# Scores of the late batches behind U, in the free columns of two PSUM banks, and five order changes

## The chip, the cores and the metric

The kernel runs on one core of a Trainium2 chip, as one launch. The metric is the device time of a run in microseconds, as the median of the runs shown. Besides that one execution was profiled: its trace holds every instruction of TensorE (PE; its weight loads are PEld), VectorE (DVE), ScalarE (ACT), GpSimd (POOL) and of the queue of SyncE (SP), with start and duration.

## The reference

Eight batches of eight heads, 576 positions of 64 values, are attended over 32 memory slots; the result goes through a gated feed-forward layer.

```python
a = exp(phi - max(phi, axis=2)); a = a / (sum(a, axis=2) + 1e-9)
k_m, v_m = einsum('bhsm,bhsd->bhmd', a, k), einsum('bhsm,bhsd->bhmd', a, v)
scores = q @ k_m.T / 8;  attn = softmax(scores, axis=-1)      # over 32 slots
x = (attn @ v_m) as (4608 tokens, 512)
out = (1 / (1 + exp(-(x @ w_gate))) * (x @ w_val)) @ w_out    # 512 -> 1536 -> 512
```

All is fp32 to the outside. Inside, the large products are made of three products of hi and lo parts.

## The kernel before

`attn @ v_m @ w` is not made in that order: for each batch, U is the product of the memory's values v_m with the weights (both gates), and what the layer needs is `attn @ U`. The feed-forward width is cut into 12 f tiles of 128. Batches 0 to 2 (below `QUAD`) run in a first part of the program, batches 3 to 7, the late ones, in a second part, batch by batch and f tile by f tile; the change lies in the second part but for `KEEP_W`. There the order of all engines is written out by hand: each call of `step` is put behind the one before it on each engine, so the order of calls in the loop over (b, f) is the order of the instructions.

For one f tile of one late batch, the object g (class `Group`) holds two gates of 288 + 288 positions, made by seven half-size products instead of eight (a scheme with sums of operands). Each product is three matmuls of 288 columns. Products 1, 6, 7 and 4 add up in one PSUM bank, called d for even f and b for odd f; product 2 goes to bank a, 5 and 3 to bank c. Of a bank's 512 columns the group uses 288. ScalarE copies partial results out of the banks (`copy`: `c_s<-d` behind product 1, `c_p<-c`, `c_x<-d`), VectorE adds (`add`: `z<-a,c_s`, `z<-c,c_x`, and the third, `z<-d,c_p` or `z<-b,c_p`, that is add(3)), ScalarE applies the sigmoid (`gate`), VectorE multiplies (`product_of`), and the result g is cut into `g_hi` (ScalarE) and `g_lo` (VectorE). One f tile later it is multiplied by w_out: an out tile is three matmuls of 512 columns into one of four accumulators, `acc`. A group's last two products, 7 and 4, are made in the next tile's step: h is the group of the tile before.

A step of the loop stands in this order on TensorE: h's product 7, g's product 1, then in even tiles U for the next two f tiles (`pair_u`, 16 matmuls in the 64*32 shape, `a<-ring,vT` and `c<-ring,vT`, into whole banks a and c, that ScalarE copies out), in some odd tiles work of the next batch (place "m"), one or two out tiles, products 2 and 5, sometimes an out tile, h's product 4, g's product 6, an out tile, product 3, an out tile. The dictionary `plan`, made by `late_sides(b)`, says what work of the next batch n = b + 1 is put at which place of which tile: `put(f, place, ...)`.

The scores of batch n are such work. Before, two pieces of 288 positions are made at f = 3 and f = 5 (place "m", `scores`), in the 64*32 shape, heads in turn into banks a and c; a piece is one part of 256 and one of 32 columns (`a<-q,kT`). VectorE transposes both banks into the tile e (`to_blocks`, place "m3"), takes the maximum over the slots (`s_max`, place "Z" of the same tile) and subtracts it (place "B" of the next). ScalarE takes the exponential of all of e at f = 6, and at f = 8 VectorE sums, inverts and multiplies (`normalize`). A tile with work at "m" is `wide`: it has two out tiles in front of product 2.

Other places that the change touches: `KEEP_W` says at which steps of the first part the converted weights are written to DRAM (two subtractions on VectorE and four DMAs on SP's queue for each entry); `leave_late` takes finished accumulators out (in batch 3 by VectorE, with rows that a DMA brings; later by ScalarE); the last step of all makes product 7 of its own group too.

Of the kernel before, what the change touches and what calls it, by code (L numbers as in the profile page):

```python
# [17 lines left out]
P = 128  # L18
B, H, S, D, M = 8, 8, 576, 64, 32
DM, DFF = 512, 1536  # L20
NG = 2
NKT = 4
NFT = DFF // P
SF = 4
# [3 lines left out]
HALF = S // 2  # L28
EDGE = TAIL // 2
HALVES = [slice(0, HALF), slice(HALF, S)]  # L30
ORDER = [list(range(H)), [2, 3, 0, 1, 6, 7, 4, 5]]
SCALE = 1.0 / 8.0
EPS = 1e-9
# [68 lines left out]
def attn_moe_kernel(  # L102
# [91 lines left out]
    def matmul(*args, **kw):  # L194
        in_turn(nc.tensor.matmul, *args, **kw)
# [274 lines left out]

    def cut(b, c):

        return slice(0, S) if c is None else (CUT if b < QUAD else HALVES)[c]

    def scores(b, c):

        n = cut(b, c).stop - cut(b, c).start
        pb = [late_bank("a"), late_bank("c")] if "banks" in pools else [bank(), bank()]
        if b < QUAD:
            parts = [(u * NKT * 2 * P, nu, 0, nu) for u, nu in PIECES[c]]  # L480
        else:
            parts = [(c * NKT * 2 * P, 2 * P, 0, 2 * P), (NKT * SF * P, TAIL, c * EDGE, EDGE)]
        o = 0
        for at_u, nu, at_c, nc_ in parts:
            qt = loaded[b, "q"][:, at_u : at_u + NKT * nu].rearrange("p (k n) -> p k n", k=NKT)
            for p in range(H):
                rs, l = of_head(b, 0, p)
                js = slice((p // 2) * M, (p // 2 + 1) * M)
                r = qt[rs, p // 2, at_c : at_c + nc_]
                matmul(pb[p % 2][js, o : o + nc_], l, r, start=True, stop=True)  # L490
            o += nc_
        loaded[b, c, "pb"] = [t[:, :n] for t in pb]

# [385 lines left out]

    spare = ident.bitcast(mybir.dt.bfloat16)  # L880
    idle = [po.tile([P, 512], F32, name=f"acc{SF - 1}")]
    memories = {b: memory(b) for b in range(QUAD)}
    is_start = {(b, f): at_start for b, f, at_start, _ in steps}

# [134 lines left out]
            yield  # L1019

    MAIN = begin[QUAD, 0]
    KEEP_W = {17: 0, 18: 1, 19: 2, 20: 3, 22: 4, 25: 5}
    sides = {
        begin[0, TURN]: [(6, remember(QUAD, True))],
        begin[1, NFT - TURN]: [(3, pause(3)), (3, score(QUAD, QUAD + 1))],
# [113 lines left out]
    def late_bank(name):  # L1139
        return pools["banks"].tile([P, 512], F32, name=name)  # L1140

    class Group:
# [19 lines left out]
        def p(self, n):  # L1162
            where, x, t, start = {
                1: ("d", "a11", "b11", True), 2: ("a", "a12", "b21", True), 5: ("c", "s1", "t1", True),
                6: ("d", "s2", "t2", False), 3: ("c", "s4", "b22", False), 7: ("d", "s3", "t3", False),
                4: ("d", "a22", "t4", False),
            }[n]
            if start:
                name = "b" if where == "d" and self.f % 2 else where
                setattr(self, where, late_bank(name)[:, :HALF])  # L1170
            self.product(getattr(self, where), x, t, start)
            if self.f == NFT - 1:
                free_rooms.append(room_of_at.pop((self.b, t)))

        def copy(self, name):
            nc.scalar.copy(getattr(self, name), self.c if name == "p5" else self.d)  # L1176

        def add(self, i):
            x, y = {0: (self.a, self.s1), 1: (self.c, self.x), 3: (self.d, self.p5)}[i]
# [132 lines left out]
    def late_sides(b):  # L1312
# [4 lines left out]
        def put(f, place, do, *args):  # L1317
            plan.setdefault((f, place), []).append((do, args))
# [5 lines left out]
        if n < B:  # L1324
            if n > QUAD + 1:
                put(0, "m2", go, n)
                put(0, "end", go, n, 2)
            soft = [s_max(n, c) for c in range(2)]
            norm = normalize(n)
            for c in range(2):  # L1330
                put(2 * c + 3, "m", scores, n, c)
                put(2 * c + 3, "m3", to_blocks, n, c)
                put(2 * c + 3, "Z", next, soft[c])
                put(2 * c + 4, "B", next, soft[c])
            put(6, "act3", s_exp, n)
            put(8, "E", next, norm)
            put(8, "Z", next, norm)
            put(9, "Z", cross, n)
            put(10, "B", sums_at, n, 1, 2)
            put(10, "act2", at_hi, n, "b11")  # L1340
            put(10, "Z", at_lo, n, "b11")
            put(11, "m", at_hi, n, "b21")
            put(11, "E", sums_at, n, 3, 4)
            put(11, "B", at_lo, n, "b21")
            put(11, "x", at_hi, n, "t1")
            put(11, "B2", at_lo, n, "t1")
            put(11, "act2", at_hi, n, "t2")
            put(11, "Z", at_lo, n, "t2")
# [39 lines left out]
    for b, f in [(b, f) for b in range(QUAD, B) for f in range(NFT)]:  # L1388
# [8 lines left out]
        odd = f % 2  # L1397
        more = n + 1 < NPAIRS
        g = Group(b, f)
        g.tiles()  # L1400
        if h:
            step(h.p, 7)
# [8 lines left out]
        wide = (b, f) in LEFT_AT and f != 5 or (f, "m") in plan and (f != NFT - 1 or b + 2 < B) or not odd and more  # L1411
        if not odd and more:
            step(pair_u, n + 1, [late_bank("c"), late_bank("a")])
            step(u_out, n + 1, "r")
            step(u_out, n + 1, "l")
        gated_late = bool(gates)
# [55 lines left out]
        if odd and more:  # L1472
            step(part_hi, n + 1, "s")
        step(g.add, 1)
        step(leave_late)
        if late_left:
            step(next, extra, None)
        last = b == B - 1 and f == NFT - 1
        if last:
            step(g.p, 7)  # L1480
            step(g.add, 3)
        if h:
            step(h.to_lo)
        side("B2")
        gates.extend([(g.gate, 0), (g.gate, 1)])
# [88 lines left out]
```

## Time and profile before

| | |
|---|---|
| median of 3 runs | 718.01 us (717.53 to 718.19) |
| the profiled execution, its own time | 717.56 us |
| span of its instructions | 715.8 us |
| TensorE, VectorE, ScalarE busy | 707.1 us (99%), 552.4 us (77%), 446.7 us (62%) |
| granted TensorE clock | 1.00 |
| chain that ended last, by engine | PE 92%, DMA 3%, ACT 2%, DVE 1% |
| loads of q, issue to landing | 16 of 512 KB, median 4.8 us |

Times in a timeline count from the span's start. A row gives start, duration, engine, line of the kernel, operation, out<-in, shape, type and count. Matmuls are pipelined, so a row's duration is longer than the time to the next start; how much TensorE a matmul takes is read from one start to the next. The same holds, by less, for VectorE and ScalarE.

### The profile page before, as it was taken

Reading aid. Unit: us, or ns where it says so; the run is one execution under the profiler, and the core shown is the slowest. Engines: PE = TensorE matmul, PEld = TensorE weight load, DVE = VectorE, ACT = ScalarE, POOL = GpSimd, SP = SyncE. Lnnn points to the kernel's source line nnn. Section 1 sums busy time; section 2 is a strip of 40 time slices with the busy share of each in tenths; the row PEclk is TensorE's granted clock in tenths of the full one; section 3 lists DMA queues with packets and bytes.
Section 4 is the critical chain, followed back from the end, with each engine's and each line's share of the span. In section 5 each row is a group of like instructions: output and inputs, shape, how many; then the busy total and the mean of one; then the engine's idle time right before and its main releaser. Section 6 shows DMA issues by size and latency. Waiting matters only on the chain.

```text
span 715.8 us, 14239 instructions
## 1 busy us (share of the span) xinstructions
PE 707.1 (99%) x5517; PEld 579.0 (81%) x5517; DVE 552.4 (77%) x1090; ACT 446.7 (62%) x1034; POOL 27.7 (4%) x55
## 2 busy tenths in 40 slices
PE   9999999999999999999999999999999999999997
PEld 7655898888988888878888888887888788888886
DVE  5898998778697675587887779777797777977663
ACT  4755776543354454567877667875777657686553
POOL 0000100111101110100000000000000000000000
PEclk9999999999999999999999999999999999999999
DMA  8966559878976535632176113652313422151102
GB/s 348 405 260 220 203 196 375 305 255 270 319 242 200 213 136 193 243 136 73 60 257 210 60 60 119 225 185 74 111 67 134 148 81 74 60 177 60 60 1 73
DMA packets 36083, 123.21 MB, mean 172 GB/s; under 512 B 3952, under 2 KB 11376, under 8 KB 28848
## 3 DMA queue, kind: packets, MB, share of 16 engines
q1 hardware_dynamic: 31296, 106.71, 42.3%
q0 software_dynamic: 4560, 15.47, 6.1%
q8 instruction: 43, 0.70, 0.4%
q14 instruction: 24, 0.20, 0.1%
q10 hardware_dynamic: 160, 0.13, 0.1%
HBM read 96.73 MB, written 25.56 MB: 171 GB/s over the span
## 4 chain that ended last, share of the span: by engine, by line
PE 92%; DMA 3%; ACT 2%; DVE 1%; SPq 1%; issue 0%; DVEq 0%; ACTq 0%
PE acc L192 39%; PE pu_t L192 20%; PE c L192 11%; PE a L192 9%; PE b L192 7%; PE d L192 7%; DMA kvm<-in_kvm_dram 2%; DMA words<-in_wo_dram 1%; SPq L178 1%; ACT L162 0%; DVE e L508 0%; DVE e L499 0%; ACT e L167 0%; ACT sg L167 0%; DVE mx L506 0%
## 5 line engine op out<-in xcount | busy, mean ns | idle before, releaser
L192 PE MATMUL acc<-wo_hi,g_hi 128*128 128x512 f32 x372 | 152.1, 409 | 0.0
L192 PE MATMUL acc<-wo_hi,g_lo 128*128 128x512 f32 x372 | 147.1, 395 | 0.0
L192 PE MATMUL acc<-wo_lo,g_hi 128*128 128x512 f32 x372 | 146.6, 394 | 0.0
L192 PE MATMUL pu_t<-at,u_hi 128*128 128x320 f32 (+1 forms) x560 | 116.5, 304 | 0.0
L192 PEld LDWEIGHTS acc<-wo_hi,g_hi 128*128 128x128 f32 x372 | 69.8, 188 | 37.5 <-ACT c_s L1176 16.8
L192 PEld LDWEIGHTS pu_t<-at,u_hi 128*128 128x128 f32 x560 | 92.1, 188 | 8.4 <-issue 2.1
L192 PEld LDWEIGHTS acc<-wo_hi,g_lo 128*128 128x128 f32 x372 | 69.8, 188 | 17.4 <-DVE g_lo L182 0.8
L192 PE MATMUL pu_t<-at,u_lo 128*128 128x256 f32 (+1 forms) x264 | 77.5, 294 | 0.0
L192 PEld LDWEIGHTS acc<-wo_lo,g_hi 128*128 128x128 f32 x372 | 70.0, 188 | 5.8
L1176 ACT COPY c_p<-c 128x288 f32<-128x288 f32 x60 | 24.0, 399 | 67.7 <-PE c L192 67.0
L167 ACT ACTIVATE sg<-pu_t 128x256 f32<-128x256 f32 (+1 forms) x70 | 28.6, 411 | 50.1 <-PE pu_t L192 45.7
L1180 DVE TENSOR_TENSOR z<-c,c_x 128x288 f32<-128x288 f32 x60 | 27.3, 456 | 34.7 <-PE c L192 31.8
L1180 DVE TENSOR_TENSOR z<-a,c_s 128x288 f32<-128x288 f32 x60 | 27.2, 453 | 34.4 <-PE a L192 32.4
L167 ACT ACTIVATE z<-z 128x288 f32<-128x288 f32 x120 | 48.1, 439 | 8.5 <-DVE z L1180 7.6
L696 DVE TENSOR_TENSOR sg<-pu_t,sg 128x320 f32<-128x320 f32 (+1 forms) x69 | 31.1, 453 | 24.8 <-ACT sg L167 14.8
L706 ACT CAST g_hi<-sg 128x256 fp32r<-128x256 f32 x66 | 26.5, 405 | 37.5 <-DVE sg L696 35.6
L192 PEld LDWEIGHTS pu_t<-at,u_lo 128*128 128x128 f32 x264 | 49.6, 188 | 0.0
L1192 ACT CAST g_hi<-z 128x512 fp32r<-128x512 f32 x60 | 37.3, 622 | 10.0 <-DVE z L1187 10.0
L182 DVE TENSOR_TENSOR g_lo<-z,g_hi 128x512 fp32r<-128x512 f32 x60 | 40.9, 682 | 1.4 <-ACT g_hi L1192 1.3
L1187 DVE TENSOR_TENSOR z<-z 128x288 f32<-128x288 f32 x60 | 27.2, 453 | 6.0 <-ACT z L167 1.1
L192 PE MATMUL a<-ring,vT 64*32 64x512 f32 x232 | 31.4, 601 | 0.0
L192 PE MATMUL c<-ring,vT 64*32 64x512 f32 x232 | 31.4, 601 | 0.0
(242 smaller groups left out, 1623.8 us busy)
## 6 DMA issues: line engine op xcount, KB each, us to landing
ring<-wgv SPq DMA_DIRECT2D x30, 1024.0 KB, 4.9
kvm<-in_kvm_dram SPq DMA_DIRECT2D x14, 1024.0 KB, 9.0
at<-at SPq DMA_DIRECT2D x18, 576.0 KB, 7.7
q<-in_qT_dram SPq DMA_DIRECT2D x16, 512.0 KB, 4.8
part<-row POOLq DMA_DIRECT2D x24, 256.0 KB, 4.9
row<-part SPq DMA_DIRECT2D x24, 256.0 KB, 3.9
words<-in_wo_dram SPq DMA_DIRECT2D x8, 512.0 KB, 9.8
words<-in_wgv_dram SPq DMA_DIRECT2D x4, 1024.0 KB, 5.1
```

The source lines that it names most:

```text
L167: last_act[0] = nc.scalar.activation(*args, **kw)
L178: last_move[queue] = queues[queue].dma_start(dst, src)
L182: return nc.vector.tensor_tensor(lo, x, hi.bitcast(F32), op=ALU.subtract)
L192: last_pe[0] = do(*args, **kw)
L696: last_prod[0] = nc.vector.tensor_tensor(prod, ps[1][:, :n], sg[:, :n], op=ALU.mult)
L706: nc.scalar.copy(hi, prod[:, : 2 * P])
L1176: nc.scalar.copy(getattr(self, name), self.c if name == "p5" else self.d)
L1180: nc.vector.tensor_tensor(self.z[:, i], x, y, op=ALU.add)
L1187: nc.vector.tensor_tensor(self.z[:, 2 + i], x, self.z[:, i], op=ALU.mult)
L1192: nc.scalar.copy(self.g[0], self.z[:, 2:4, : 2 * P])
```

## The change

The scores of batches 4 to 7 (n above `QUAD`) are cut into three pieces of 224, 224 and 128 positions (`ROOMFULS`), since a bank has 224 free columns beside a group's 288. They are made at f = 2, 4 and 6, at a new place "u" directly behind `pair_u`, heads in turn into the free columns of the bank of the tile before (b) and of this tile (d); `now` holds the two groups, and `beside` is the free part of a group's bank. These matmuls don't start an accumulation (`start=False`). Positions 224 to 448 lie over the border of the two halves, so the second piece has three parts (32, 32 and 160 columns), the third two (96 and 32). Tiles 3 and 5 are no longer `wide`. The maximum comes at "Z" of the same tile, the subtraction at "B" of the next, the exponential in two parts at f = 6 and 7.

The five order changes: the weights of pair 4 are kept at step 27 instead of 22; the copy `c_s` of f = 7 in batch 3 is made by VectorE; the product by the inverse sums goes from "Z" of f = 8 to "E" of f = 9 in batch 6; in batch 3 the lo part of h is made ahead of the rows that leave; and in the last step it is made ahead of the last third sum.

```diff
+ROOM = 512 - HALF
+ROOMFULS = [slice(o, min(o + ROOM, S)) for o in range(0, S, ROOM)]
...
     def cut(b, c):
-        return slice(0, S) if c is None else (CUT if b < QUAD else HALVES)[c]
+        if c is None or isinstance(c, slice):
+            return c or slice(0, S)
+        return (CUT if b < QUAD else HALVES if b == QUAD else ROOMFULS)[c]
...
-        pb = [late_bank("a"), late_bank("c")] if "banks" in pools else [bank(), bank()]
+        late = b > QUAD
+        pb = [unit.beside for unit in now] if late else [bank(), bank()]
...
-            parts = [(c * NKT * 2 * P, 2 * P, 0, 2 * P), (NKT * SF * P, TAIL, c * EDGE, EDGE)]
+            parts, cs = [], cut(b, c)
+            for k, half in enumerate(HALVES):
+                edge = half.stop - EDGE
+                for at_u, nu, first, a, z in (
+                    (k * NKT * 2 * P, 2 * P, 0, half.start, edge), (NKT * SF * P, TAIL, k * EDGE, edge, half.stop),
+                ):
+                    lo, hi = max(a, cs.start), min(z, cs.stop)
+                    if lo < hi:
+                        parts.append((at_u, nu, first + lo - a, hi - lo))
...
-                matmul(pb[p % 2][js, o : o + nc_], l, r, start=True, stop=True)
+                matmul(pb[p % 2][js, o : o + nc_], l, r, start=not late, stop=True, skip_group_check=late)
...
-    KEEP_W = {17: 0, 18: 1, 19: 2, 20: 3, 22: 4, 25: 5}
+    KEEP_W = {17: 0, 18: 1, 19: 2, 20: 3, 25: 5, 27: 4}
...
-                setattr(self, where, late_bank(name)[:, :HALF])
+                whole = late_bank(name)
+                setattr(self, where, whole[:, :HALF])
+                if where == "d":
+                    self.beside = whole[:, HALF:]
...
-            nc.scalar.copy(getattr(self, name), self.c if name == "p5" else self.d)
+            late_exp = name == "s1" and self.b == QUAD and self.f == 7
+            copy = nc.vector.tensor_copy if late_exp else nc.scalar.copy
+            copy(getattr(self, name), self.c if name == "p5" else self.d)
...
-            for c in range(2):
-                put(2 * c + 3, "m", scores, n, c)
-                put(2 * c + 3, "m3", to_blocks, n, c)
-                put(2 * c + 3, "Z", next, soft[c])
-                put(2 * c + 4, "B", next, soft[c])
-            put(6, "act3", s_exp, n)
+            for c in range(len(ROOMFULS)):
+                put(2 * c + 2, "u", scores, n, c)
+                put(2 * c + 2, "m3", to_blocks, n, c)
+                put(2 * c + 2, "Z", next, soft[c])
+                put(2 * c + 3, "B", next, soft[c])
+            put(6, "act3", s_exp, n, slice(0, 2 * ROOM))
+            put(7, "act3", s_exp, n, 2)
             put(8, "E", next, norm)
-            put(8, "Z", next, norm)
+            put(*((8, "Z") if m < B else (9, "E")), next, norm)
...
         g = Group(b, f)
+        now[:] = [now[1], g]
...
             step(pair_u, n + 1, [late_bank("c"), late_bank("a")])
+            side("u")
             step(u_out, n + 1, "r")
...
         step(g.add, 1)
+        to_lo_done = h and b == QUAD and leaving
+        if to_lo_done:
+            step(h.to_lo)
         step(leave_late)
...
         if last:
+            step(h.to_lo)
             step(g.p, 7)
             step(g.add, 3)
-        if h:
+        elif h and not to_lo_done:
             step(h.to_lo)
```

TensorE in batch 4 at f = 2, behind U, in the changed program; the waits name the engine's count that a matmul waits for (DVE is VectorE's, Activation ScalarE's, DMAHW a DMA queue's):

```order
L194 MATMUL c<-ring,vT 32x512
L194 MATMUL a<-ring,vT 32x512
L194 MATMUL b<-q,kT 32x224 [waits DMAHW0_49,DVE_49]
L194 MATMUL d<-q,kT 32x224 [waits Activation_49]
L194 MATMUL b<-q,kT 32x224
L194 MATMUL d<-q,kT 32x224
L194 MATMUL b<-q,kT 32x224
L194 MATMUL d<-q,kT 32x224
L194 MATMUL b<-q,kT 32x224
L194 MATMUL d<-q,kT 32x224
L194 MATMUL acc_4834<-wo_hi,g_hi 128x512
```

Before, the out product stood directly behind U, and the scores stood in the next tile. The counts waited for are those of the third sum of the tile before (`z<-b,c_p`) and of the copy `c_s<-d`.

VectorE in batch 3 from f = 1 to f = 2, before, and then after:

```order
L1180 TENSOR_TENSOR z<-c,c_x 128x288 [waits PE_49,Activation_49]
L756 TENSOR_TENSOR row<-acc_3397,row 128x512 [waits DMAHW3_49,DMASW1_49]
L756 TENSOR_TENSOR row<-acc_3401,row 128x512 [waits DMAHW4_49,DMASW2_49]
L182 TENSOR_TENSOR g_lo<-z,g_hi 128x512 [waits Activation_49]
L182 TENSOR_TENSOR u_lo<-s_raw,u_hi 128x768 [waits Activation_49]
L1180 TENSOR_TENSOR z<-b,c_p_3699 128x288 [waits PE_49]
```

```order
L1199 TENSOR_TENSOR z<-c,c_x 128x288 [waits PE_49,Activation_49]
L184 TENSOR_TENSOR g_lo<-z,g_hi 128x512 [waits Activation_49]
L769 TENSOR_TENSOR row<-acc_3397,row 128x512 [waits DMAHW3_49,DMASW1_49]
L769 TENSOR_TENSOR row<-acc_3401,row 128x512 [waits DMAHW4_49,DMASW2_49]
L184 TENSOR_TENSOR g_lo<-z,g_hi 128x512 [waits DVE_49]
L184 TENSOR_TENSOR u_lo<-s_raw,u_hi 128x768 [waits Activation_49]
L1199 TENSOR_TENSOR z<-b,c_p_3699 128x288 [waits PE_49]
```

One g_lo is added in front of the two rows, and the one behind them is still there.

VectorE in batch 4 from the end of f = 3 into f = 4, before, and then after:

```order
L1180 TENSOR_TENSOR z<-c,c_x 128x288 [waits PE_49,Activation_49]
L182 TENSOR_TENSOR g_lo<-z,g_hi 128x512 [waits Activation_49]
L182 TENSOR_TENSOR s_lo<-s_raw,s_hi 128x768 [waits Activation_49]
L506 TENSOR_REDUCE mx<-e 128x2x9
L1180 TENSOR_TENSOR z<-b,c_p_4861 128x288 [waits PE_49]
L1187 TENSOR_TENSOR z<-z 128x288 [waits DVE_49,Activation_49]
```

```order
L1199 TENSOR_TENSOR z<-c,c_x 128x288 [waits PE_49,Activation_49]
L184 TENSOR_TENSOR g_lo<-z,g_hi 128x512 [waits Activation_49]
L184 TENSOR_TENSOR s_lo<-s_raw,s_hi 128x768 [waits Activation_49]
L1199 TENSOR_TENSOR z<-b,c_p_4893 128x288 [waits PE_49]
L512 STREAM_TRANSPOSE e<-b 128x224 [waits PE_49]
L512 STREAM_TRANSPOSE e<-d 128x224 [waits PE_49,Activation_49]
```

The maximum in front of the third sum is gone from here (it stands at the end of f = 2, 4 and 6 now), and two transposes follow the sum.

## Rows read from the trace of the kernel before

**Rows 1.** The page: an engine's busy time, share of the span, instructions.

```profile
PE 707.1 (99%) x5517; PEld 579.0 (81%) x5517; DVE 552.4 (77%) x1090; ACT 446.7 (62%) x1034; POOL 27.7 (4%) x55
```

**Rows 2.** Timeline, TensorE, batch 4, f = 3: one piece of the scores.

```profile
390.58 0.43 PE L192 MATMUL b<-at,u_hi 128*128 128x288 f32 x2
390.85 0.29 PE L192 MATMUL b<-at,u_lo 128*128 128x288 f32 x1
391.08 0.40 PE L192 MATMUL a<-q,kT 64*32 64x256 f32 x1
...
391.53 0.19 PE L192 MATMUL a<-q,kT 64*32 64x32 f32 x1
...
391.73 0.50 PE L192 MATMUL acc<-wo_hi,g_hi 128*128 128x512 f32 x1
392.07 0.40 PE L192 MATMUL acc<-wo_lo,g_hi 128*128 128x512 f32 x1
```

**Rows 3.** Timeline, all engines, batch 4, f = 2: U, third sum, copy.

```profile
384.30 0.61 PE L192 MATMUL c<-ring,vT 64*32 64x512 f32 x1
...
384.83 0.45 DVE L1180 TENSOR_TENSOR z<-b,c_p 128x288 f32<-128x288 f32 x1
385.16 0.40 ACT L1176 COPY c_s<-d 128x288 f32<-128x288 f32 x1
```

**Rows 4.** Timeline, all engines, batch 4, f = 4: U and VectorE's maximum.

```profile
397.50 0.61 PE L192 MATMUL c<-ring,vT 64*32 64x512 f32 x1
...
398.03 0.75 DVE L506 TENSOR_REDUCE mx<-e 128x18 f32<-128x576 f32 x1
```

**Rows 5.** Timeline, all engines, batch 4, f = 6: U and VectorE's maximum.

```profile
413.52 0.61 PE L192 MATMUL c<-ring,vT 64*32 64x512 f32 x1
...
414.65 0.74 DVE L506 TENSOR_REDUCE mx<-e 128x18 f32<-128x576 f32 x1
```

**Rows 6.** Timeline, all engines, batch 3, end of f = 1 into f = 2.

```profile
303.41 0.62 ACT L1192 CAST g_hi<-z 128x512 fp32r<-128x512 f32 x1 [0.78 <-DVE z L1187]
...
303.76 1.28 DVE L756 TENSOR_TENSOR row<-acc,row 128x512 f32<-128x512 f32 x2
...
304.02 0.61 PE L192 MATMUL c<-ring,vT 64*32 64x512 f32 x1
...
304.95 0.68 DVE L182 TENSOR_TENSOR g_lo<-z,g_hi 128x512 fp32r<-128x512 f32 x1
...
305.55 0.95 DVE L182 TENSOR_TENSOR u_lo<-s_raw,u_hi 128x768 fp32r<-128x768 f32 x1
...
306.42 0.45 DVE L1180 TENSOR_TENSOR z<-b,c_p 128x288 f32<-128x288 f32 x1
```

**Rows 7.** Timeline, TensorE, batch 3, f = 7.

```profile
339.79 0.29 PE L192 MATMUL d<-at,u_lo 128*128 128x288 f32 x1
340.14 0.53 PE L192 MATMUL b<-at,u_hi 128*128 128x288 f32 x2
```

**Rows 8.** Timeline, all engines, batch 6, f = 9.

```profile
607.88 0.45 DVE L1180 TENSOR_TENSOR z<-d,c_p 128x288 f32<-128x288 f32 x1
608.02 0.40 PE L192 MATMUL acc<-wo_hi,g_lo 128*128 128x512 f32 x1
608.38 0.53 PE L192 MATMUL d<-at,s_hi 128*128 128x288 f32 x2
```

**Rows 9.** Timeline, TensorE, batch 7, last step.

```profile
702.63 0.39 PE L192 MATMUL acc<-wo_hi,g_hi 128*128 128x512 f32 x1
702.86 0.39 PE L192 MATMUL acc<-wo_lo,g_hi 128*128 128x512 f32 x1
703.27 0.50 PE L192 MATMUL acc<-wo_hi,g_lo 128*128 128x512 f32 x1
```

**Rows 10.** Timeline: VectorE, a weight subtraction; SP's queue, q's loads of batch 5.

```profile
220.10 0.68 DVE L1226 TENSOR_TENSOR row<-wg 64x512 f32<-64x512 f32 x1 [0.60 <-DMA part<-row]
...
378.89 1.28 SPq L178 DMA_DIRECT2D q<-in_qT_dram  x3
```

More of the change, by code (lines that the diff above doesn't have):

```diff
@@ L881, in attn_moe_kernel @@
     idle = [po.tile([P, 512], F32, name=f"acc{SF - 1}")]
+    now = [None, None]
     memories = {b: memory(b) for b in range(QUAD)}
@@ L1327, in late_sides @@
                 put(0, "end", go, n, 2)
-            soft = [s_max(n, c) for c in range(2)]
+            soft = [s_max(n, c) for c in range(len(ROOMFULS))]
             norm = normalize(n)
-            for c in range(2):
-                put(2 * c + 3, "m", scores, n, c)
-                put(2 * c + 3, "m3", to_blocks, n, c)
-                put(2 * c + 3, "Z", next, soft[c])
-                put(2 * c + 4, "B", next, soft[c])
-            put(6, "act3", s_exp, n)
+            for c in range(len(ROOMFULS)):
[5 more added lines that the diff above has]
+            put(7, "act3", s_exp, n, 2)
             put(8, "E", next, norm)
-            put(8, "Z", next, norm)
+            put(*((8, "Z") if m < B else (9, "E")), next, norm)
             put(9, "Z", cross, n)
```

## The prediction

> **What bounds the kernel now.** I read the page first: the reader is to see that TensorE is busy for 99% of the span while VectorE and ScalarE are not [rows 1], and, in the table, that the chain of work that ended last runs almost wholly through TensorE. Then TensorE's timeline inside batches 3 to 7, the part that the change touches. There the matmuls stand back to back: a 288-column one starts 0.13 us after the last (390.58 to 390.85 for two), a 512-column one 0.23 us after it [rows 2, 9]. So time is gained only where TensorE is made to do less or to wait less, and every wait that is added on TensorE is paid in full, since the matmuls behind it are taken in the program's order. Two kinds of loss are seen in the rows. One is the trip into the 64*32 shape and back. The other is a handful of places where the next matmul starts late because VectorE or ScalarE is late [rows 7 to 9]; there the matmul behind the late one loses another 0.10 us (0.53 for the pair instead of 0.43, and 0.50 instead of 0.39).
>
> **The scores leave their own trips.** Before, one piece of the scores costs TensorE the time from 390.98 (390.85 and 0.13) to 391.84 (392.07 less 0.23), 0.86 us [rows 2, 9]; a batch has two, 1.72. After, the three pieces stand behind U, which is in the same shape, so they pay no entry (390.98 to 391.08, 0.10), no exit and no loss behind it. What stays is the streaming: 256 columns take 0.45 for both passes, so 576 take 1.01. A part of 32 columns costs more than its columns: 391.53 to 391.73 is 0.20, 0.10 without an exit like the entry, against 0.06 by columns; three such parts (before: two) add 0.13. So 1.14 instead of 1.72, 0.58 a batch, and 2.3 us for the four batches (4 to 7). Bounds: three short parts at 0.20 each leave 1.1 us of gain; none of the surcharge makes it 2.8.
>
> **What the scores wait for now.** This is the term that decides. The pieces are written into the free columns of banks d and b, and the built program makes the first matmul into each wait, as the rows in the section on the change show: for b on a VectorE count, which is the third sum of the group before (`z<-b,c_p`), for d on a ScalarE count, which is the copy `c_s<-d`. Both only read the first 288 columns, but the wait is there, and behind the waiting matmul stand all out products of the tile. Before, U was followed by out products that needed neither. So the question at each of the twelve places (four batches, f of 2, 4, 6) is whether those two are done when U ends. U is two rounds of 512 columns, 0.90 by the rate above. A release takes 0.05 (the sum that starts at 607.88 ends at 608.33, and the matmul that waits for it starts at 608.38) [rows 8].
> - f = 2, batch 4: U starts at 384.30 and ends at 385.20; the sum ends at 385.28, the copy, late behind the copies of the finished rows, at 385.56 [rows 3]. Wait until 385.61: 0.41 us.
> - f = 4, batch 4: U ends at 398.40. The sum stood behind a maximum; that maximum now comes a tile earlier, so the sum starts where it started, at 398.03, and ends at 398.48 [rows 4]. Wait 0.13 us.
> - f = 6, batch 4: U ends at 414.42. Here VectorE also copies the leftover sums ahead of it. Without the maximum the sum starts at 414.65 and ends at 415.10 [rows 5]. Wait 0.73 us.
> - Batches 5 and 6 repeat these three places with the same distances; 1.27 us a batch, 3.8 for three.
> - f = 2, batch 3: here VectorE adds the finished rows of batch 2. The edit that puts the lo part of g ahead of them does so, but its guard is the list of rows itself, which is empty by the time that it is asked again, so the old lo part stays as well: VectorE does it twice, as the order shows. The chain: g_hi is there at 304.03, the first lo part starts at 304.08 and takes 0.60 (304.95 to 305.55), the two rows 1.19 (303.76 to 304.95), the second lo part 0.60, the lo part of U 0.87 (305.55 to 306.42), the sum 0.45 [rows 6]. It ends at 307.78, and TensorE may start at 307.83; U ends at 304.92. Wait 2.9 us.
> - f = 4 and 6, batch 3: a maximum goes as in rows 4, and there are no leftovers; 0.13 each.
> Sum: 2.9, 0.3 and 3.8, so 7.0 us. What a wait costs beyond itself no row shows for this shape; it lies between nothing and the 0.10 seen for full-size matmuls [rows 7, 8], for twelve places 0 to 1.2. I take 0.4, nearer to nothing, since the loads in the 64*32 shape are short and the shape doesn't change.
>
> The built program waits by bank. The Trainium skill has the rule for it, in PSUM — Partial Sum Buffer, section "PSUM bank collisions raise a hardware error": two engines must be kept apart by bank and quadrant, a different address in the same bank still collides. No row of the kernel before shows two engines in one bank at once. By that rule the waits can't be left out, and the time is the forecast's; if columns alone counted, it would be the first rival's.
>
> **The other edits.** The copy on VectorE (f = 7 of batch 3) takes away the wait at 340.14: 0.22 (339.92 to 340.14) and 0.10 behind it [rows 7]; VectorE is not late there. Moving the product by the inverse sums one step on, behind the sum `z<-d,c_p` that it held up, takes away the wait at 608.38: 0.13 and 0.10 [rows 8]. The lo part ahead of the last third sum takes away that at 703.27: 0.18 (703.09 to 703.27) and 0.11 [rows 9]. Together 0.84 us, if all go; 0 if what comes next is as late. The exponential in two parts adds one short instruction to ScalarE, at f = 7, where it is ahead of the tile's sigmoids by a table load: 0. The 16 further small VectorE instructions (transposes and maxima) stand between waits for TensorE, on an engine that is 77% busy: 0. The weights kept at step 27 instead of 22 move two VectorE subtractions of 0.68 [rows 10] and four DMAs on SP's queue. TensorE shows no wait at the old place, so nothing is gained; at the new one they lengthen a busy run of VectorE by 1.2 us, of which TensorE sees between 0 and 1.2. I take 0, as a lag of three halves is between the two engines there. On SP's queue the DMAs now stand ahead of batch 3's loads of q and of two sets of row loads, whose users come a tile or more later: 0. In the late batches q is needed a tile earlier: issued at 378.89 [rows 10], its first piece, the only one that f = 2 reads, has 6.3 us until 385.20, and the median load takes 4.8 (table): 0.
>
> **The sum.** From the profiled execution's own 717.56: less 2.3, less 0.84, plus 7.0, plus 0.4 gives 721.8, 4.3 us more. The median of the runs, 718.01, lies 0.45 above the profiled execution; I put half of that on top: 722.0 us.
>
> **The rivals.**
> 1. The free columns are free in time: the sum and the copy end before U does, so no wait shows and the gains alone stand: 718.0 less 3.1, 714.9 us. For it: at f = 4 the sum is late by a tenth only, and anything that makes VectorE 0.15 us quicker or TensorE later hides that. Against it: at f = 6 it is late by 0.7 and at batch 3 by 2.9, and VectorE's chain starts when TensorE's last product into c ends, so it is late by the same amount however TensorE is delayed. It decides where the `z<-b,c_p` ends ahead of U's last matmul. Chance 0.10.
> 2. Only the long wait of batch 3 remains, and the others are hidden: the gains of 3.1 and the loss of 2.9 cancel, 717.9 us. It needs the copies of finished rows at f = 2 and the leftovers at f = 6 to fall elsewhere than before; the order shows them at the same places. Chance 0.08.
> 3. The waits cost more than themselves: each re-pays 0.10 (1.2 in all), and VectorE's subtractions at step 27 reach TensorE: 723.5 to 724.5 us. Chance 0.14.
> 4. The forecast: waits as worked out, 720 to 723.4 us. Chance 0.68.
>
> **How the numbers follow.** This kernel's runs differ by 0.2%, 1.4 us, so that is what I call no change. Slower by more than that holds the forecast nearly whole and the third rival: 0.80. No change is the second rival and the edge of the forecast: 0.10. Faster is the first rival: 0.10. The range holds 8 in 10 if it reaches from 717.2 (just under the second rival) to 724.2 (the third's upper part); what it leaves out is the first rival and a little above. The forecast's own range is 720 to 723.4.
>
> **What would show it.** In TensorE's timeline of the changed kernel: the first matmul of `b<-q,kT` starts late behind U's last, by some 2.9 us in batch 3 at f = 2, 0.4 at f = 2 of the other batches (the second one, into d, there), 0.1 at f = 4 and 0.7 at f = 6, each just behind the end of `z<-b,c_p` or `c_s<-d`; two g_lo in a row of four on VectorE in batch 3; no 64*32 matmuls at odd f; and U to the next out product without a second entry. The waits at 340, 608 and 703 are gone. I am wrong if the score matmuls start within 0.05 of U's end at most places, if the gain of the trips is not near 0.58 a batch, or if a wait of over 0.5 us shows at a place that I didn't name.

## The result, and the profile after

| | before | after |
|---|---|---|
| median of the runs | 718.03 us (717.53 to 718.19, 4 runs) | 726.56 us (725.42 to 726.89, 4 runs) |
| the profiled execution, span | 717.56 us, 715.8 us | 726.36 us, 724.6 us |
| second U of the late part (batch 3, f = 0) to the span's end | 422.31 us | 431.31 us |
| granted TensorE clock | 1.00 | 0.998 |

The ratio is 1.0123, 95% interval 1.0111 to 1.0135: slower, as forecast, but by 8.5 us and not by 4.0, above the top of the range (724.2). The third row of the table is what I compare kernels by below. The opening moves single executions by up to 1.2 us (that U starts between 293.0 and 294.2 us in the kernels of this study), while the same program repeats the rest within a few hundredths (420.72 and 420.74 in two profiles of one kernel).

The page of the changed kernel, busy time and the chain that ended last:

```profile
PE 708.6 (98%) x5645; PEld 580.2 (80%) x5645; DVE 556.2 (77%) x1108; ACT 446.1 (62%) x1037; POOL 27.6 (4%) x55
...
PE 85%; DVE 7%; DMA 3%; ACT 3%; issue 1%; SPq 1%; DVEq 0%
```

Beside [rows 1], TensorE is busy for 1.5 us more, which is not the 8.8 that the span grew by: the rest is waiting. The chain says for whom: VectorE's share went from 1% to 7%. The view of waits names it, TensorE's waits from 303 to 620 us (waited for: us in total, times, longest); the same view of the kernel before has no line:

```profile
PE b L194 <- DVE z L1199: 6.7, 9, 2.7
```

Nine of the twelve score places wait for the third sum. The three others, f = 2 of batches 4 to 6, wait in the second matmul, for the copy, and don't show in this view. Here are the places of batches 3 and 4, in the timelines that answer to [rows 3 to 6].

Batch 3, f = 2, TensorE and then VectorE (start, duration, engine, line, operation; a trailing bracket is idle time and its releaser):

```profile
303.85 0.61 PE L194 MATMUL c<-ring,vT 64*32 64x512 f32 x1
...
307.67 0.37 PE L194 MATMUL b<-q,kT 64*32 64x224 f32 x1 [2.73 <-DVE z L1199]
...
308.21 0.51 PE L194 MATMUL acc<-wo_hi,g_hi 128*128 128x512 f32 x1
```

```profile
303.89 0.69 DVE L184 TENSOR_TENSOR g_lo<-z,g_hi 128x512 fp32r<-128x512 f32 x1 [0.22 <-ACT g_hi L1211]
304.50 1.28 DVE L769 TENSOR_TENSOR row<-acc,row 128x512 f32<-128x512 f32 x2
305.69 0.68 DVE L184 TENSOR_TENSOR g_lo<-z,g_hi 128x512 fp32r<-128x512 f32 x1
306.29 0.95 DVE L184 TENSOR_TENSOR u_lo<-s_raw,u_hi 128x768 fp32r<-128x768 f32 x1
307.16 0.45 DVE L1199 TENSOR_TENSOR z<-b,c_p 128x288 f32<-128x288 f32 x1
```

The row of [rows 6] with one g_lo more, as forecast: the sum ends at 307.61, the scores start 0.06 later, 2.9 us after U's end at 304.75.

What I had not forecast stands behind that wait. TensorE by stretches (length, busy, granted clock, DMA share, GB/s), and two matmuls of the stretch:

```profile
304.00:306.80 2.80, 0.94 (x16) 1.00 0.35 38
306.80:309.00 2.20, 1.33 (x19) 0.98 0.93 305
309.00:310.00 1.00, 1.00 (x4) 0.50 0.70 250
...
312.00:313.00 1.00, 1.00 (x8) 0.84 0.00 0
```

```profile
309.09 0.63 PE L194 MATMUL acc<-wo_hi,g_hi 128*128 128x512 f32 x1
309.52 0.63 PE L194 MATMUL acc<-wo_lo,g_hi 128*128 128x512 f32 x1
```

The granted clock is the lower of its two levels, 1.2 instead of 2.4 GHz, from about 308.9 to 312.3 us, and a 512-column matmul takes 0.43 from start to start there, not 0.23.

Batch 4, f = 4, VectorE from the end of f = 3, and then TensorE:

```profile
399.76 0.61 DVE L521 TENSOR_TENSOR e<-e,mx 128x448 f32<-128x448 f32 x1
400.29 0.45 DVE L1206 TENSOR_TENSOR z<-d,z 128x288 f32<-128x288 f32 x1
...
401.43 0.69 DVE L184 TENSOR_TENSOR g_lo<-z,g_hi 128x512 fp32r<-128x512 f32 x1 [0.32 <-ACT g_hi L1211]
402.31 0.96 DVE L184 TENSOR_TENSOR s_lo<-s_raw,s_hi 128x768 fp32r<-128x768 f32 x1 [0.19 <-ACT s_hi L1136]
403.18 0.45 DVE L1199 TENSOR_TENSOR z<-b,c_p 128x288 f32<-128x288 f32 x1
```

```profile
401.86 0.61 PE L194 MATMUL c<-ring,vT 64*32 64x512 f32 x1
...
403.69 0.21 PE L194 MATMUL b<-q,kT 64*32 64x32 f32 x1 [0.74 <-DVE z L1199]
...
404.45 0.50 PE L194 MATMUL acc<-wo_hi,g_hi 128*128 128x512 f32 x1
```

In [rows 4] the maximum started 0.53 after U, and I let the sum start there. It starts 1.32 after U (403.18 less 401.86), and the scores wait 0.93, not 0.13. The new row in this stretch is the subtraction at 399.76. The same stretch of the kernel before, where U starts at 397.50, has none:

```profile
394.87 0.45 DVE L1187 TENSOR_TENSOR z<-d,z 128x288 f32<-128x288 f32 x1
396.19 0.46 DVE L1180 TENSOR_TENSOR z<-c,c_x 128x288 f32<-128x288 f32 x1 [0.86 <-PE c L192]
```

The gate product `z<-d,z` starts 2.63 ahead of U there and 1.57 ahead of it now, so 1.06 later against U. What hangs on it runs through ScalarE: g_hi reads it, s_hi stands behind g_hi in ScalarE's order, and VectorE's g_lo and s_lo read those two; the third sum stands behind s_lo. The last link before the change, and g_hi now:

```profile
396.03 0.83 ACT L1122 CAST s_hi<-s_raw 128x768 fp32r<-128x768 f32 x1
397.16 0.95 DVE L182 TENSOR_TENSOR s_lo<-s_raw,s_hi 128x768 fp32r<-128x768 f32 x1
```

```profile
400.77 0.62 ACT L1211 CAST g_hi<-z 128x512 fp32r<-128x512 f32 x1 [0.98 <-DVE z L1206]
```

Before, s_hi ended at 396.86, 0.30 ahead of the s_lo that reads it: that was the room of this chain. Now g_hi waits for the gate product, g_lo for g_hi and s_lo for s_hi (0.98, 0.32 and 0.19), and the sum comes 0.79 later (1.32 for 0.53). The 0.86 us that VectorE was idle in front of `z<-c,c_x` is no measure of that room: there it waited for TensorE, and the chain doesn't run through it.

Batch 4, f = 2, TensorE and ScalarE, and f = 6, TensorE and VectorE, as forecast from [rows 3, 5]:

```profile
388.69 0.61 PE L194 MATMUL c<-ring,vT 64*32 64x512 f32 x1
...
389.73 0.56 PE L194 MATMUL b<-q,kT 64*32 64x224 f32 x2
390.01 0.37 PE L194 MATMUL d<-q,kT 64*32 64x224 f32 x1
```

```profile
389.55 0.40 ACT L1195 COPY c_s<-d 128x288 f32<-128x288 f32 x1
```

```profile
420.24 0.27 PE L194 MATMUL b<-q,kT 64*32 64x96 f32 x1 [0.54 <-DVE z L1199]
```

```profile
417.68 0.68 DVE L831 COPY wo_raw<-a 128x512 f32<-128x512 f32 x1
...
419.74 0.45 DVE L1199 TENSOR_TENSOR z<-b,c_p 128x288 f32<-128x288 f32 x1
```

At f = 2 the first matmul into d starts 0.06 after the end of the copy (389.95). At f = 6 the leftover sums' copy still stands ahead of g_lo, the lo part and the sum; the sum ends at 420.19, and the scores start 0.05 later, 0.73 after U's end (U starts at 418.62).

### The profile page after: what moved, and what is told of

The parts are those of the page before. It is cut to its first block, busy times and chain, and to the rows that moved or that the text cites. A ratio compares the mean times of both kernels' runs of the same rounds, so it can differ in the third digit from the quotient of the medians.

```text
span 724.6 us, 14507 instructions
## 1 busy us (share of the span) xinstructions
PE 708.6 (98%) x5645; PEld 580.2 (80%) x5645; DVE 556.2 (77%) x1108; ACT 446.1 (62%) x1037; POOL 27.6 (4%) x55
## 4 chain that ended last, share of the span: by engine, by line
PE 85%; DVE 7%; DMA 3%; ACT 3%; issue 1%; SPq 1%; DVEq 0%
PE acc L194 36%; PE pu_t L194 20%; PE c L194 9%; PE a L194 8%; PE b L194 6%; PE d L194 6%; DMA kvm<-in_kvm_dram 2%; DVE z L1199 1%; DMA words<-in_wo_dram 1%; DVE s_lo L184 1%; DVE u_lo L184 1%; ACT g_hi L1211 1%; SPq L180 1%; DVE e L521 1%; ACT s_hi L1136 1%
```

## The experiments

All are compared by the time from the second U to the end (before 422.31, after 431.31 us), which comes from one profiled execution of each kernel, with the medians beside it. Medians of the kernel before on these chips were 717.3 to 717.6 us.

**The subtraction back in the even tile.**

```diff
-                put(2 * c + 3, "B", next, soft[c])
+                put(2 * c + (4 if c < 2 else 3), "B", next, soft[c])
```

> The changed kernel, but the subtraction of the maximum of the first two score pieces stands in the next even tile (f = 4 and 6, where it stood before the change) and no longer in the odd tile (f = 3 and 5), ahead of the odd tile's gate product. Theory 1 (order on VectorE): in the odd tile the subtraction, 0.61 us, pushes back the chain gate product, g_hi, g_lo, s_lo, third sum, so that at f = 4 the scores wait 0.48 or 0.93 us instead of 0.13. Without it the third sum starts at U + 0.53, the first b<-q,kT at U + 1.03, at f = 4 of batches 3 to 6 and f = 6 of batch 3; three times 0.35 and twice 0.80, so 2.65 us less: 723.9. Theory 2 (more and smaller VectorE instructions, the transposes and maxima of three pieces, make it late): the waits stay at 0.48 and 0.93 and the time at 726.5 within 0.4.

Measured: 724.76 us (ratio to before 1.0101, 1.0082 to 1.0121), 429.48 us, 1.83 less than after. Half a hit. VectorE in batch 4 from f = 3 to f = 4, U at 401.67:

```profile
399.56 0.45 DVE L1206 TENSOR_TENSOR z<-d,z 128x288 f32<-128x288 f32 x1
...
402.47 0.45 DVE L1199 TENSOR_TENSOR z<-b,c_p 128x288 f32<-128x288 f32 x1
```

The gate product comes 0.54 earlier against U (2.11 ahead of it) and the sum starts 0.80 after U instead of 1.32. But it does not come back to 0.53: the wait is 0.40 at f = 4 of batches 3 to 5, and 0.13 only at f = 6 of batch 3 and f = 4 of batch 6. So the subtraction is most of it. For the rest the rows show two things in f = 2: at its end the first piece's maximum (0.61) now stands behind the maximum over positions of the batch after next, which batch 6 does not have; and the sum of product 2, which started 3.19 us after U in the kernel before, starts 3.94 after it here, since the piece and its wait now stand ahead of product 2. Neither was tried alone.

**The lo part of batch 3 made once.**

```diff
-        to_lo_done = h and b == QUAD and leaving
+        to_lo_done = bool(h and b == QUAD and leaving)
```

> The changed kernel, with the guard of the lo part in batch 3 read once as true or false, so that g_lo is made once there, ahead of the rows, and not again behind them. Theory 1: the wait of the scores at f = 2 of batch 3 is VectorE's row of four; one g_lo less makes it 2.3 us instead of 2.9, and the granted clock behind it still falls: 725.9. Theory 2: the clock falls only behind a wait as long as 2.9; then the half-rate stretch behind it goes too, another 1.7 less: 724.2. Theory 3: the second g_lo is hidden (the sum waits for something else): 726.5.

Measured: 726.4 us (1.0125, 1.0105 to 1.0144), 431.09 us, only 0.22 less. At f = 2 the first theory is right: the wait is 2.3 us, f = 2 to f = 4 takes 0.62 less (16.62 for 17.24), and the clock falls all the same:

```profile
306.80:309.00 2.20, 2.13 (x20) 0.64 0.87 305
309.00:310.00 1.00, 1.00 (x4) 0.50 0.88 336
```

One place on, 0.41 is given back: the scores at f = 4 of batch 3 wait 0.93 instead of 0.48. I read it so: while TensorE stands still, VectorE works off its backlog, and a shorter stop leaves it later at the next.

**The first piece of batch 4 at f = 3** (beside the lo part made once).

```diff
-                put(2 * c + 2, "u", scores, n, c)
-                put(2 * c + 2, "m3", to_blocks, n, c)
-                put(2 * c + 2, "Z", next, soft[c])
-                put(2 * c + 3, "B", next, soft[c])
+                late_one = n == QUAD + 1 and c == 0
+                put(2 * c + 2 + late_one, "act" if late_one else "u", scores, n, c)
+                put(2 * c + 2 + late_one, "act" if late_one else "m3", to_blocks, n, c)
+                put(2 * c + 2 + late_one, "Z", next, soft[c])
+                put(2 * c + 3 + late_one, "B", next, soft[c])
```

> The changed kernel with the lo part of batch 3 made once (as in the run before) and, beside it, batch 4's first score piece (made in batch 3) put one tile later, f = 3 behind the out tile, in a trip of its own, so that nothing on TensorE waits for the third sum at f = 2 of batch 3. Theory 1 (the half-rate stretch from 309 us is a result of the wait): wait and half rate both vanish, U to U from f = 2 to f = 4 of batch 3 goes from 16.6 us to 13.2, the granted clock is 1.00 throughout: 3.4 less than with the lo part alone, 722.9 where the kernel before takes 718.0. Theory 2 (the half rate comes from something else at that place): the wait goes, the clock still falls, 1.4 of it stays: 724.3.

Measured: 723.47 us (1.0084, 1.0072 to 1.0096), 428.43 us, 2.66 less than with the lo part alone. Without the wait the clock stays:

```profile
308.00:310.00 2.00, 2.00 (x15) 1.00 1.00 311
```

The DMA share (1.00) is as high as in the changed kernel, so the transfers alone do not lower the clock. From f = 2 to f = 4 it takes 13.84 and not 13.2 us: the piece's own trip, a new wait of 0.31 for g_lo at 312.17, and one of the piece itself for a third sum (0.20 of idle time in front of it).

**The lo part of U's sums behind the third sum.**

```diff
         if h:
             step(h.add, 3)
+        if not odd and n:
+            step(part_lo, n, "s")
         step(g.copy, "s1")
...
-        if odd and more:
-            step(part_lo, n + 1, "s")
         if f > 1 or b > QUAD:
```

> The changed kernel with one VectorE instruction moved: the lo part of U's sums (128x768, 0.95 us), made at the end of every odd tile ahead of the third sum, stands right behind that sum, so the third sum is 0.87 earlier at every even tile. Nothing else differs. Theory 1 (the scores wait for the third sum, and the sum for its place in VectorE's row): at f = 6 of batches 4 to 6 the wait 0.73 goes (2.2 in all); at f = 4 the copy c_s is what is left: 0.93 becomes 0.53 in batches 4 and 5, 0.48 becomes 0.1 in the others and at f = 6 of batch 3 (1.9 in all); at f = 2 of batch 3 2.9 becomes 2.0 (0.9): 5.0 less than 726.5, 721.5, and 720.1 if after 2.0 the clock does not fall. Theory 2 (what is late is the lo part itself or what stands ahead of both): product 5, which reads the lo part, now waits instead, or the copy c_s holds the scores up as long: not below 724.5.

Measured: 720.22 us (1.0042, 1.0026 to 1.0057), 424.71 us, 6.60 less than after, with one instruction put behind another; some 1.4 of it is the half clock of batch 3, which this profile does not have. It is the first theory, and its second number. VectorE and TensorE at f = 6 of batch 4, beside the rows of after above:

```profile
415.24 0.68 DVE L184 TENSOR_TENSOR g_lo<-z,g_hi 128x512 fp32r<-128x512 f32 x1
415.84 0.45 DVE L1199 TENSOR_TENSOR z<-b,c_p 128x288 f32<-128x288 f32 x1
416.20 0.95 DVE L184 TENSOR_TENSOR u_lo<-s_raw,u_hi 128x768 fp32r<-128x768 f32 x1
```

```profile
415.58 0.61 PE L194 MATMUL c<-ring,vT 64*32 64x512 f32 x1
...
416.46 0.24 PE L194 MATMUL b<-q,kT 64*32 64x96 f32 x1
```

The scores start 0.88 after U's start, with no wait, and product 5 is not held up. In batch 3 the wait is 2.1 us, and behind it the clock stays at 1.00 in the profiled execution; two of the six executions, at 721.94 and 722.25 us, have a mean clock of 0.997 and 0.998, as the changed kernel has:

```profile
306.99 0.37 PE L194 MATMUL b<-q,kT 64*32 64x224 f32 x1 [1.85 <-DVE z L1199]
```

```profile
306.80:309.00 2.20, 2.01 (x22) 1.00 0.81 261
309.00:310.00 1.00, 1.00 (x9) 1.00 0.91 303
```

**Other cuts: 160 and 384.**

```diff
-ROOMFULS = [slice(o, min(o + ROOM, S)) for o in range(0, S, ROOM)]
+ROOMFULS = [slice(0, 160), slice(160, 384), slice(384, S)]
...
-            put(6, "act3", s_exp, n, slice(0, 2 * ROOM))
+            put(6, "act3", s_exp, n, slice(0, ROOMFULS[1].stop))
```

> The changed kernel with the pieces cut at 160 and 384 instead of 224 and 448, so that the second piece has parts of 96, 32 and 96 columns instead of 32, 32 and 160, and the third 160 and 32 instead of 96 and 32: four short parts a batch become two or three, with the same 576 columns. Theory 1: a 32-column part costs some 0.10 us beyond its columns, two in a row more, which is why a batch's scores gained 0.38 and not 0.58: some 0.15 us less a batch, 0.6 in all: 726.0. Theory 2: the missing gain is in entering and leaving (per piece): no change, 726.5.

Measured: 727.24 us (1.0129, 1.0110 to 1.0149); 430.59 us, 0.72 less than after, about the first theory's 0.6; the median, 727.24 for 726.56, doesn't show it. But the reason is another, and the total alone would have misled me. The middle piece with parts of 96, 32 and 96 columns takes from its first matmul to the next out product 0.76 us, as with 32, 32 and 160 (404.45 less 403.69 above):

```profile
403.10 0.27 PE L194 MATMUL b<-q,kT 64*32 64x96 f32 x1 [0.48 <-DVE z L1199]
...
403.86 0.51 PE L194 MATMUL acc<-wo_hi,g_hi 128*128 128x512 f32 x1
```

It only starts 0.26 earlier against U (which starts at 401.53 here), as on VectorE the maximum and the subtraction of a first piece of 160 take 0.48 and 0.49 us instead of 0.61 each. So the parts' shortness is not the price; their number may be (three in both).

**The order changes alone**, on the kernel before: the change's edits of `KEEP_W`, `copy`, the place of the product by the inverse sums and the last step, word for word, and the lo part of batch 3 made once.

```diff
-    KEEP_W = {17: 0, 18: 1, 19: 2, 20: 3, 22: 4, 25: 5}
+    KEEP_W = {17: 0, 18: 1, 19: 2, 20: 3, 25: 5, 27: 4}
...
+            late_exp = name == "s1" and self.b == QUAD and self.f == 7
+            copy = nc.vector.tensor_copy if late_exp else nc.scalar.copy
...
-            put(8, "Z", next, norm)
+            put(*((8, "Z") if m < B else (9, "E")), next, norm)
...
+        to_lo_done = bool(h and b == QUAD and leaving)
+        if to_lo_done:
+            step(h.to_lo)
         step(leave_late)
...
```

> The kernel before the change with the five order changes alone (scores in two pieces in banks a and c as before; the lo part in batch 3 made once). Theory 1: the three waits at 340, 608 and 703 us vanish and nothing takes their place: 0.84 less, 717.2. Theory 2: an order change costs as much as the others bring (the weights kept at step 27 make a wait at 229 us, or the lo part ahead of the rows holds up what the rows free): 718.0.

Measured: 717.4 us, 0.9996 (0.9984 to 1.0008); 421.72 us, 0.59 less than before. The medians can't tell it from no change. In the trace, the wait at 340 [rows 7] goes (0.31 less from f = 6 to f = 8 of batch 3) and that at 703 [rows 9] (0.23). That at 608 [rows 8] goes too, 0.22 from f = 8 to f = 10 of batch 6, but 0.20 comes back within the next two stretches, where waits that the kernel before has too grow longer: that in front of the product at 626.99 us in batch 7 by 0.09 (0.43 behind the out product's start, before 0.34). The reading is that the product by the inverse sums now stands in front of later work on VectorE; it was not tried without.

**All covers together**, and the same with batch 4's first piece left behind U. Beyond the edits above (lo part once, subtraction in even tiles, lo part of the sums behind the third sum, first piece at f = 3) the sigmoids of f = 1 stand behind the copy c_s of f = 2 in batches 4 to 7:

```diff
+        while gates and f == 2 and b > QUAD:
+            step(*gates.pop(0))
...
-        while gates and not (f == 7 and b + 1 < B):
+        while gates and not (f == 7 and b + 1 < B or f == 1 and b > QUAD):
```

> All covers together: the changed kernel with the lo part in batch 3 made once, the subtractions back in even tiles, the lo part of U's sums behind the third sum, batch 4's first piece at f = 3 in a trip of its own, and in batches 4 to 7 the sigmoids of f = 1 behind the copy c_s of f = 2. Theory 1 (the scores behind U are worth 0.38 us a batch once nothing waits, and the order changes 0.6): no b<-q,kT starts later than U + 0.95, batches 4 to 6 gain 0.38 each and batch 3 0.1: 716.1 where the kernel before takes 718.0. Theory 2 (VectorE and ScalarE have no room, the moved work is late for its next reader): new waits at product 5 or at the out tiles behind U, 717.5 or more.

> As the run with all covers, but batch 4's first piece stays directly behind U of f = 2 in batch 3, where VectorE still has g_lo and two rows ahead of the third sum. Theory 1: a wait of 1.4 us there, and the granted clock falls behind it as behind 2.9 and 2.3: 1.1 and 1.4 more than with all covers, 718.6. Theory 2: 1.4 is too short for the clock to fall: 717.2.

Measured: all covers 715.91 us, 0.9977 (0.9967 to 0.9987), 420.72 us, 1.59 less than before. A second time, on one chip with the same order without the scores' move (told below; the expectation calls it the run above), 716.76 us, 0.9989 (0.9979 to 0.9999), 420.74:

> The run with all covers, beside the one above on the same chip. Theory 1: 1.1 us below the run above, 1.4 to 1.9 below the kernel before. Theory 2: the two within 0.3 of each other.

With batch 4's first piece left behind U 716.76 us, 0.9992 (0.9980 to 1.0004), 421.53: a wait of 1.5 us there, and the clock stays at 1.00 in the profile. With all covers no score behind U waits; TensorE in batch 4 at f = 2, 4 and 6, where U starts at 384.05, 396.76 and 412.63:

```profile
384.05 0.61 PE L194 MATMUL c<-ring,vT 64*32 64x512 f32 x1
...
384.93 0.35 PE L194 MATMUL b<-q,kT 64*32 64x224 f32 x1
...
385.45 0.50 PE L194 MATMUL acc<-wo_hi,g_hi 128*128 128x512 f32 x1
```

```profile
397.64 0.19 PE L194 MATMUL b<-q,kT 64*32 64x32 f32 x1
...
398.48 0.50 PE L194 MATMUL acc<-wo_hi,g_hi 128*128 128x512 f32 x1
```

```profile
413.51 0.24 PE L194 MATMUL b<-q,kT 64*32 64x96 f32 x1
...
413.98 0.50 PE L194 MATMUL acc<-wo_hi,g_hi 128*128 128x512 f32 x1
```

Without scores the out product comes 1.02 after U's start; here 1.40, 1.72 and 1.35. So the pieces cost 0.38, 0.70 and 0.33, 1.41 a batch for the 1.72 of two trips [rows 2]: the gain is 0.31, not 0.58.

**The same order without the scores' move**: the kernel before, the order changes and the lo part of the sums behind the third sum, so to the diff of the order changes these lines:

```diff
+        if not odd and n:
+            step(part_lo, n, "s")
         step(g.copy, "s1")
...
-        if odd and more:
-            step(part_lo, n + 1, "s")
```

> The kernel before the change with the five order changes and the lo part of U's sums behind the third sum, the scores in two pieces in banks a and c as before. It asks what of the gain of the run with all covers (715.9 where the kernel before takes 717.4 on that chip) is the scores' place. Theory 1: the scores' place, 0.31 us in each of batches 4 to 6 and 0.18 at f = 4 and little else in batch 3, so about 1.1; then this run is 0.6 faster than the kernel before (the order changes and the waits at 626 and 636 us): 717.2 by the first shared median of 717.8, and the run with all covers stays the faster one. Theory 2: the order on VectorE brought it all: 716.2 or less by the same median.

Measured: 716.5 us, 0.9992 (0.9982 to 1.0003), 421.38 us. That is 0.93 less than before, more than the 0.6 expected, and 0.65 more than with all covers. The medians of the two on this chip, 716.5 and 716.76, do not show that difference: 1.1 in favour of all covers was the first theory of their comparison, and by the medians the second one, within 0.3, is what came. The scores' place is read from the traces alone. There 0.14 of the 0.65 is one wait of U at f = 6 of batch 5 that no other profile has; what is left is some 0.5 us: 0.31 in each of batches 4 to 6, less 0.46 in batch 3, whose first piece not only takes a trip of its own, as each piece did before, but waits in it for the third sum (it could have started at 311.33). With all covers:

```profile
311.70 0.37 PE L194 MATMUL d<-q,kT 64*32 64x224 f32 x1 [0.20 <-DVE z L1199]
```

**Batch 4's scores as before, the rest covered.** `late` and the cuts in three hold for b > QUAD + 1; batch 4 has its two pieces at f = 3 and 5:

```diff
-        late = b > QUAD
+        late = b > QUAD + 1
...
+            old = n == QUAD + 1
-            for c in range(len(ROOMFULS)):
+            for c in range(2 if old else 3):
+                put(2 * c + 2 + old, "m" if old else "u", scores, n, c)
...
```

> The run with all covers, but the scores of batch 4 (made in batch 3) are made as before the change, in two pieces at f = 3 and 5 in banks a and c; only batches 5 to 7 have theirs behind U. In batch 3 the run with all covers lost 0.27 us from f = 2 to f = 4, gained 0.18 in the next stretch and had nothing left of the 0.31 that the copy c_s of f = 7 gives back. Theory 1 (what a batch gains or loses is settled by its own places): batch 3 takes 0.36 us less than before the change instead of 0.11 more, so from the second U to the end 0.47 less than with all covers, 420.25 us, 2.06 less than the kernel before; the time 0.997 to 0.998 of it. Theory 2 (a batch's lateness is carried on): 420.7, no better.

Measured: 715.34 us (714.67 to 716.08), 0.9967 (0.9955 to 0.9979), 420.41 us, 1.90 less than before and near the first theory's 420.25: the fastest version of the study, faster than the kernel before by 0.33%. About half of it (0.93, the run above) comes without moving any score.

## Why the prediction was wrong

The direction and the place were right, and the size was not. Priced at the next out product against the run with all covers, the sum of 9.0 us (second U to the end) splits into 9.4 of waits and 1.4 of half clock, less 1.24 (four batches by 0.31) and 0.59 for the order changes: 9.0. Step by step:

1. **The step that failed: "f = 4, batch 4: ... the sum starts where it started", wait 0.13 us.** The five places priced so (f = 4 and f = 6 of batch 3, f = 4 of batches 4 to 6) cost 0.43, 0.43, 0.88, 0.88 and 0.43, so 3.0 instead of 0.65. I had asked what is removed ahead of the sum (the maximum) and not what is added one tile earlier on the same engine: by the diff the subtraction moves from "B" of an even to "B" of an odd tile, where it stands ahead of the gate product. I had put such instructions at 0, "between waits for TensorE, on an engine that is 77% busy". The 77% says nothing at this place: the chain from the gate product over ScalarE to the sum had 0.30 us of room in batch 4, and the gate product came 1.06 later, 0.53 of it by the subtraction. The first experiment and that with the lo part show it from two sides; what makes the rest of the 1.06 was not tried alone. None of the rivals had this step, though it is the largest part of the 4.7 us by which the forecast was short (9.0 for 4.3).
2. **What the long wait costs beyond itself**: I bounded it by 0 to 0.10 a place, from rows of short waits. At eleven places this holds; behind the 2.9 us of batch 3 the half clock took 1.4 us more (f = 2 to f = 4 grew by 3.87: 2.96 of wait and 0.38 for the piece, less the 0.86 of the old one, leave 1.39). In the profiles with that wait gone, or 2.1 us long, it is not seen.
3. **The gain of the trips** was 1.24 instead of 2.3, just inside the lower bound of 1.1, and a gain "not near 0.58 a batch" was one of the prediction's signs of being wrong. One part of 224 columns costs what the columns cost (0.38, forecast 0.39). Three parts of together 224 cost 0.70, so each further part some 0.16 (two parts of together 128 cost 0.33, some 0.10 over their columns), where I took 0.04 over its columns from a 32-column row. What in a change of part costs this is not settled; the other cuts only say that it is not the parts' shortness.
4. **The wait of 2.9 in batch 3, those of 0.41 at f = 2 and 0.73 at f = 6** were right (3.0; 0.46; 0.66 to 0.68), in place and cause.
5. **The order changes** gave 0.59, not 0.84: most of the wait at 608 comes back in the next two stretches (and 0.59 is read from traces; the medians show no change). That the weights kept at step 27 cost nothing holds to within the opening's own spread.
6. Of the rivals, the third came nearest (waits dearer than themselves), but by the clock and not by VectorE's work at step 27. The first one, in which the banks are free in time, is answered by the traces: at the nine places the scores start 0.05 or 0.06 after the sum's end. Sum and scores use different columns, but the program waits by bank; a program that waits by columns was not run. The Trainium skill, PSUM — Partial Sum Buffer, section "PSUM bank collisions raise a hardware error", asks for accesses of two engines kept apart by bank and quadrant, different columns or not; the program's waits keep to that, and no run here shows what two engines in one bank at once would do.

## What to carry to other kernels

When an instruction moves by one tile, look at both ends: who is freed where it stood, and what is queued behind it where it now stands, down to the engine that sets the end. Read the slack of that chain link by link from the rows at that place, from the end of what an instruction reads to its start, over all engines that the chain runs through; neither the engine's busy share over the span (77%) nor an idle bracket beside the chain (0.86 us here, where the chain had 0.30) gives it. And where a matmul must wait for a small instruction, first ask whether that instruction can go ahead of a large one that nobody waits for yet: one such exchange was worth 6.6 us of the 9.0 that the change lost here (with it alone the kernel was still 2.4 us slower than before; it gained only with the other covers).

## What the runs showed of the hardware

The granted clock went to 0.50 around the end of waits of 2.3 and 2.9 us in which TensorE did nothing, from 0.1 us ahead of the end to 1.3 behind it (four profiles: after, the subtraction back, the lo part once, the other cuts). It stayed at 1.00 in the profiles behind waits of 1.5 and 2.1 us (one each) and without a wait, with transfers as dense under way. Its price was 1.3 to 1.4 us on top of the wait. It is not certain either way: of the 21 executions of those four kernels, 18 have a mean granted clock of 0.998 or less, and three of 0.999 or more, each the fastest of its kernel; at 0.998 or less are also two of six executions with the wait of 2.1 us, one of ten with that of 1.5, and 7 of the 74 of the kernel before that ran beside the experiments. What decides it in one execution is not shown here. The Trainium skill's TensorE: Matmul & The Clock Gate, Part 1, names the two levels and idleness as what lowers the clock; the four profiles agree in that.
